# A new order for every operation of an attention + feed-forward kernel, and a last PSUM bank that is split

## The chip, the cores and the metric

The kernel runs on one core of a Trainium2 chip. The metric is the device time of one execution in microseconds (us): 369.22 us is the median of three runs of the kernel before (368.81, 369.22 and 369.6). One more execution was profiled; its own time was 369.51 us.

Names used below: TensorE (PE in the profile) multiplies matrices, its weight loads are PEld; VectorE is DVE, ScalarE is ACT, GpSimd is POOL, SyncE is SP. PSUM is the memory that TensorE writes, in banks of 2 KB per partition; SBUF is the large on-chip memory; HBM is off the core. A DMA moves data between HBM and SBUF and is issued from an engine's queue.

## The reference

```python
# attention, B=8 batches, H=12 heads, S=448 rows, D=64 columns per head
scores = (1/8) * q @ k.T
attn   = relu(scores)**2 / 448
y      = attn @ v                                   # [8, 12, 448, 64]
x      = y.transpose(0, 2, 1, 3).reshape(3584, 768)
# feed-forward, w_in [768, 2048], w_out [2048, 768]
h      = x @ w_in
g      = 0.5 * h * (1 + erf(h / sqrt(2)))           # exact gelu
out    = g @ w_out                                  # [3584, 768], float32
```

Inputs are float32 in HBM; matrices are cast to bf16 by the loads (or by a copy, for the first blocks), and sums are kept in float32 in PSUM.

## The kernel before, in words

**The work.** For each batch there are four kinds of TensorE work.

- *Transposes* (`T`): q and k come with their rows on the partitions and are wanted with D on the partitions. For batches 0 and 1 TensorE does this (`add_tk`, `add_tq`) into a bank `tp`, which ACT or DVE copies to SBUF. For batches 2 to 7 it is done by DMA transposes that are issued from SP's queue (`add_T_dma`); each waits for its load and for all scores of the batch two before, whose buffer it fills. Per batch there are three groups of four heads, and per group three transposes: k, the even and the odd part of q (called k, e and o below: T3.0k is batch 3, group 0, k).
- *Attention* (`A`): a score step (`add_steps`, 21 per batch) is four matmuls of 64x64 tiles into a two-bank tile `ps`; ACT or DVE applies the scaled relu, and DVE squares it into `a_sq`. Seven steps feed one value product (`add_av`, 28 matmuls of 64x64 tiles into `pav`, three per batch), which two copies put into `xT`.
- *W_in* (`F`): `add_f1` makes one block of 128 hidden columns for one batch, six matmuls of 128x128 tiles by 448 columns into `psh`, and ACT applies gelu. There are 16 blocks for each of batches 0 to 4. The last three batches use a form with seven products in place of eight (`add_blocks`, tiles `pb`, sums on DVE at L1028 into `part`). W_in is loaded in five pieces of 2, 2, 4, 4 and 4 blocks (win0 to win4), each by three DMAs; block 8 is the first of win3.
- *W_out* (also `F`): two tiles of 128 rows are done plainly (`add_plain`); the rest are 13 groups of 256 rows (`add_group`), again with seven products, p1 to p7, of eight matmuls by 384 columns each into three banks a, b, c of one pool. Products that follow each other in one bank accumulate, and between them DVE (or ACT) passes a partial sum out: in bank b p6, p7, p4 lead to v2, v3 and c21; in bank c p5 leads to c22 and p3 to c12. c21 and c22 are the left and right half of the second 128 rows, c11 and c12 those of the first. `store_rows` writes a tile of 128 rows to HBM in one or two DMAs.

**PSUM.** `w_pp` has three tiles of two banks (tag "w"; `ps` and `pav`), `f_pp` two tiles of one bank (tag "f"; everything else).

**The order.** Every operation, load and transpose is recorded as an `Op` with its dependencies. A string, `ORDER` (L83), then lists all of them: each word is an engine (P TensorE, A ACT, D DVE, G GpSimd's queue, S SyncE's queue) and the number of the op. `place` (L351) walks the string and issues each op on that engine, so the string settles the order on every engine and queue, and for copies and relus also which of ACT and DVE does them. A word Z issues a zero product (`add_fill`), which only keeps TensorE running. Before the order begins TensorE runs `SPIN` zero matmuls of 512 columns.

**Loads and gates.** All loads but the first two tiles are issued from GpSimd's queue. From batch 3 on a load reuses the buffer of the batch before; a *gate* (`add_gate`), a small GpSimd copy that reads the result of a group's transposes, stands ahead of the loads that overwrite what these transposes read. The start of the load order is

```text
k0.1 q0.1a v0.0 k0.2 [ident] q0.2a v0.1 v0.2 q0.b win0 win1 k1.0 q1.0 v1.0 win2
k1.1 q1.1 v1.1 win3 k1.2 q1.2 v1.2 win4 k2.0 q2.0 v2.0 k2.1 ...
```

Here k0.1 is k of batch 0, heads of group 1; q0.1a is the first half of the columns of q; q0.b the second half for all groups; [ident] is no load but the making of the identity matrix for TensorE's transposes, also on GpSimd. Later the gates of a batch alternate with loads: gate3.0 k4.0 q4.0 gate3.1 k4.1 q4.1 gate3.2 and so on.

Of the kernel before, what the change touches and what calls it, by code (L numbers as in the profile page):

```python
# [8 lines left out]
F32 = mybir.dt.float32  # L9
# [18 lines left out]
ND = DM // 2  # L28
# [51 lines left out]
SPIN = 9  # L80
# [3 lines left out]
G0 G1 G2 G3 G1429 G4 G5 A10 P11 D13 A16 G6 P17 D12 P14 D18 G7 P42 P39 P19 A15 G8 P21 D43 P33 D44  # L84
P36 A40 A22 D20 P54 P25 A37 P23 G9 D34 P51 D26 P48 A55 Z1024 D35 A24 D56 P69 Z672 D41 G117 A49
P57 D38 A52 P63 D70 P45 A58 D53 P66 D50 A64 P27 G118 A46 P31 D59 P60 D28 A67 D32 A47 P78 D65 P29
A61 P81 G119 D68 D30 A79 D62 G120 P93 P108 D71 A82 P84 A94 P75 D109 P72 G121 D83 A85 P90 D80
P129 G122 D73 A76 P105 A74 P102 G123 D95 D130 A91 G124 P131 D86 A106 P141 D77 D132 A103 D92 P111
P96 P165 D104 P143 A112 D107 D113 A97 P156 P87 D98 G125 A166 P99 D110 G126 A157 D88 P114 A142
G127 A89 D100 A101 P174 P168 G128 A144 P133 D115 P135 A116 P171 D175 P159 A169 D134 P251 D136  # L90
A160 D170 P145 D158 A172 A252 D167 P162 D176 P186 P192 A146 P243 D161 G147 D173 A187 G148 P253
A163 D193 G149 A244 D164 P195 G150 P180 P198 A254 P137 P139 G151 A181 D196 P183 P177 D138 A199
D140 A184 P189 P219 P245 D178 A190 D185 P247 D194 A220 G152 D179 A246 G153 P213 D188 P222 P204
D221 A248 G154 P263 D197 G155 A214 D200 P265 D191 A205 A264 D182 P261 A223 A266 D224 P216 P207
P201 S231 D206 A262 A208 P210 S229 P259 D209 A217 D215 P255 S232 D211 A260 P249 D212 D218 A256
D202 P225 A203 S228 A250 P257 A226 S230 P267 D227 A258 S234 P348 A268 P350 S233 G237 G238 A349
P352 G239 S235 A351 P354 S236 A353 P288 P294 P282 A355 P358 D289 P356 D283 A359 P360 D295 A357
D290 D296 P306 G240 A361 P279 G241 P276 P362 D307 P364 D280 A363 P366 D277 A365 P368 A367 P370
A369 P300 P285 P291 A371 P372 A292 D286 P374 D284 A373 P318 D301 P303 P312 A375 D308 P376 G242
G269 A304 D319 P378 G270 D278 A377 G271 P380 D313 G272 A379 D293 G273 D314 G274 P382 D390 A381  # L100
D305 D302 G275 D391 P330 P309 D287 D281 S398 P297 A331 D392 D320 S399 P315 P384 A298 D393 S401
A310 D396 A383 D417 P387 D394 A385 D419 A299 D311 A316 D395 P324 D317 P321 D418 A325 D397 P333
A388 P327 P421 D420 D322 S400 A328 P423 D323 A334 D326 S386 D422 P339 S402 P336 P342 D424 P425
D329 G407 G408 S403 A343 D335 P427 G409 A426 D337 S389 P429 A340 S404 D428 D344 P431 S405 D338
D341 P440 D332 P437 P345 D430 A438 D441 G410 P443 G411 P446 D432 P433 S406 A346 G412 D347 A444
P509 A447 D434 P511 D439 S435 D448 A510 S436 D442 P449 P452 P455 S541 D562 A512 P513 D445 A453
P515 D454 A450 A514 S542 P517 D456 G413 G414 D451 G415 P464 D457 S543 P461 P458 G416 A465 D462
A518 P467 P470 A516 P519 A459 P521 D471 A520 D472 P523 D466 A468 D460 A522 D560 P479 P476 P473
D469 A524 P525 D463 A477 P527 D480 A474 S544 D478 A526 P529 D475 A528 D481 P488 P485 P482 A489
D486 S545 A530 P494 P491 G550 P531 G551 D487 D483 G552 S546 P533 D495 A532 A484 P535 S547 D496  # L110
D561 A492 D490 A534 P503 P500 P497 D493 A536 P537 P564 D498 A538 D504 P539 A501 S548 D499 G553
A565 D505 G554 P600 D502 P603 G555 P506 S549 A601 D604 A540 P606 P609 P566 D563 A507 D602 P568
D607 D567 P570 D610 A569 A508 P572 G556 D571 G557 P624 P612 G558 P618 S704 P574 D580 G559 D608
A613 D573 P576 S705 A619 D581 D582 P627 D575 S706 P615 P584 D614 D577 A616 D611 P586 D605 A628
D617 A625 D620 P636 P630 A585 P621 D629 A631 D637 P633 P588 D587 A622 D626 D623 A634 S578 P639
P642 D583 P648 S707 P590 D638 G713 A640 D635 G714 A589 S579 D632 P592 G715 D641 A643 S708 D591
A649 P651 P657 D644 P645 S709 D593 A652 P666 D658 S710 P654 P594 D653 A646 D659 A655 D650 P596
A647 D667 D595 P660 P766 P663 D597 P672 A661 S711 D767 G716 P674 G717 A664 D662 A673 G718 D656
S712 P676 D668 A675 D665 S598 P772 P769 P669 S599 A770 D773 P763 A677 P775 P678 S867 D670 A764
D771 P680 D723 A776 D768 A679 S868 P790 A671 D765 P778 G719 P781 G720 A681 D777 P682 G721 S869  # L120
D791 P684 G722 D725 A683 P686 D779 A782 A685 D783 P688 D780 D774 P787 P793 D724 P784 A788 D794
A687 P799 P796 A689 P690 D795 D789 A797 P692 D798 A691 S870 P694 A693 A785 P696 A695 A786 P698
A800 S871 G876 A697 P802 G877 P811 D801 P805 A699 P700 G878 S872 A803 D812 P702 D792 A806 S873
D804 P814 D807 P817 P808 A815 D818 A701 P823 P820 A703 D816 P727 D809 A821 D726 P729 A810 D819
S874 A728 G879 D822 G880 D813 P826 A824 P829 G881 P906 S875 D730 P731 A830 D827 P733 A907 D828
D831 D825 P912 P921 P832 D745 A913 A732 P909 D922 P924 P735 D734 A833 A925 G882 P737 G883 A910
D743 G884 A834 D914 P936 P918 G885 P933 D736 P739 D738 S741 D744 A934 S978 P747 D908 A937 D740
S742 A919 D938 P749 S979 D935 A748 D926 P942 P930 S980 P915 D750 P751 A931 D943 P753 D920 A916
A752 D746 P755 D923 D911 D944 P948 P945 D917 P927 D888 S981 A949 D754 P939 D950 P757 A928 D886
D756 A946 P759 S982 D887 A940 D758 A929 P835 D932 S983 D947 D941 P957 P954 P951 S984 A836 A955  # L130
D958 P960 S985 P963 D760 P837 D959 A961 D952 S761 P839 D956 A953 S986 A838 D964 P966 P972 P969
D962 A840 P841 S762 D889 A973 D965 P843 A842 D967 P847 A970 A844 D971 P845 D968 D974 P990 P987
D1067 P975 A991 D988 A846 P993 P996 A848 D992 P849 A976 D1068 D1070 P851 A997 D989 A850 P853
A994 A977 D995 A852 P1005 P1002 P999 A854 P855 A1003 D1006 P859 D1004 A1000 D998 A856 P857 D1007
D1001 P1011 P1014 P1008 D1059 A858 A1012 D1015 P1017 P1026 P861 A1009 D1063 A860 P863 D1060
A1018 D1010 A1027 P1020 D1061 P1029 A862 P1023 P865 D1016 A864 D1019 A1021 D1028 P890 D1022 A866
P892 D1062 A1024 D1013 A891 D1025 P894 A1030 D1069 D893 D1031 P1035 P1038 P1032 A895 D1064 A1036
D1066 P1041 A1039 D1037 P1044 P896 D1033 A1042 D1034 A1045 P898 D1040 D1043 D897 P1047 D1046
P1050 P1053 D899 P900 D1139 A1048 D1049 P902 A1051 D1140 A1054 D1052 P1071 D1055 P1056 D901 S904
A1072 D903 S905 D1141 P1088 P1073 D1057 P1090 A1089 D1058 P1143 D1074 P1075 D1091 P1092 A1144  # L140
D1065 P1077 D1142 P1094 A1076 D1179 P1079 A1093 D1180 P1096 D1078 P1145 D1095 D1080 P1082 D1097
A1081 D1181 P1099 A1098 D1146 P1085 P1102 D1083 P1105 D1100 A1084 P1122 D1086 A1101 P1107 D1103
A1087 P1124 D1182 A1106 A1123 P1147 A1104 D1108 P1109 D1125 P1126 A1148 P1111 P1128 A1110 P1113
A1127 P1130 D1112 P1149 D1129 D1114 P1116 D1131 A1115 P1133 A1132 D1150 P1119 P1136 D1117 P1151
D1134 A1118 D1120 A1135 P1153 D1137 A1121 D1291 A1138 D1292 D1152 P1155 D1159 D1154 S1157 P1163
D1160 D1156 S1158 P1165 D1161 D1164 P1167 D1162 D1166 D1293 P1169 D1294 A1168 P1171 D1170 P1173
D1253 D1172 P1175 D1251 D1174 S1177 P1183 D1252 P1200 D1176 S1178 P1185 D1254 P1202 A1184 A1201
P1255 D1186 P1187 D1203 P1204 A1256 P1189 P1206 A1188 P1191 A1205 P1208 D1190 P1257 D1207 D1192
P1194 D1209 A1193 P1211 A1210 D1258 P1197 P1214 D1195 P1217 D1212 A1196 P1234 D1198 A1213 P1219
D1215 A1199 P1236 A1218 A1235 P1259 A1216 D1220 P1221 D1237 P1238 A1260 P1223 P1240 A1222 P1225  # L150
A1239 P1242 D1224 P1261 D1241 D1226 P1228 D1243 A1227 P1245 A1244 D1262 P1231 P1248 D1229 P1263
D1246 A1230 D1232 A1247 P1265 D1249 A1233 A1250 D1264 P1267 D1271 D1266 S1269 P1275 D1272 D1268
S1270 P1277 D1273 D1276 P1279 D1274 D1278 P1281 D1280 P1283 D1282 P1285 D1365 D1284 P1287 D1363
D1286 S1289 P1295 D1364 P1312 D1288 S1290 P1297 D1366 P1314 A1296 A1313 P1367 D1298 P1299 D1315
P1316 A1368 P1301 P1318 A1300 P1303 A1317 P1320 D1302 P1369 D1319 D1304 P1306 D1321 A1305 P1323
A1322 D1370 P1309 P1326 D1307 P1329 D1324 A1308 P1346 D1310 A1325 P1331 D1327 A1311 P1348 A1330
# [1378 lines left out]
```

## Time and profile before

| | |
|---|---|
| median of 3 runs | 369.22 us (368.81 to 369.6) |
| the profiled execution's own time | 369.51 us |
| its span in the trace | 367.7 us |
| mean granted TensorE clock | 0.993 |
| PE busy | 357.6 us, 97% of the span |
| PEld, DVE, ACT, POOL busy | 219.9, 285.4, 199.6, 64.4 us |
| last TensorE product ends | 362.6 us |
| last DMA lands | 366.5 us |

How to read it: all times inside the trace count from the span's start. The execution's time is 1.81 us above its span; 1.18 us of the span lie behind the last landing. A product whose results go on to DVE or ACT is free for them some 0.4 us after the end that the trace gives for its last matmul. Three stages follow one another in the span: the first 31 us, in which loads, transposes and the first batch's attention start up; up to about 249 us, in which attention of one batch and feed-forward work of earlier ones alternate on TensorE; and the rest, in which only feed-forward work is left.

### The profile page before, as it was taken

The numbers are of one execution on the slowest core, as the hardware profiler recorded it, in microseconds if no ns is written. First come the engines' busy times: TensorE is split into PE (matmuls) and PEld (weight loads), VectorE is DVE, ScalarE is ACT, GpSimd is POOL, SyncE is SP. The second block draws the span as 40 slices with busy tenths as digits, with TensorE's granted clock in tenths as the row PEclk, the third lists the DMA queues.
The fourth block names the chain that finished last, engine by engine and source line by source line (L and its number), as shares of the span: only waits on it lengthen the run. The fifth ranks groups of instructions, "written<-read, shape, count | busy, mean of one in ns | idle before, by whom it ended". The sixth has DMA issues, their size and how long they took to land.

```text
span 367.7 us, 8379 instructions
## 1 busy us (share of the span) xinstructions
PE 357.6 (97%) x3525; PEld 219.9 (60%) x3525; DVE 285.4 (78%) x473; ACT 199.6 (54%) x319; POOL 64.4 (18%) x103
## 2 busy tenths in 40 slices
PE   7899999999999999999999999999999999999995
PEld 3676644455554455545455544558875897688663
DVE  4898863699888889989598997998788558665862
ACT  5898954436467546775777568863540353045200
POOL 8566404140113240230402000000000000000000
PEclk9899999999999999999999999999999999999998
DMA  9999999999999999999998990002002301210323
GB/s 175 192 181 202 203 199 157 195 203 197 165 214 244 153 186 210 224 184 146 150 130 147 193 180 11 0 2 87 3 0 87 86 2 51 87 37 0 87 86 86
DMA packets 89540, 47.25 MB, mean 128 GB/s; under 512 B 55328, under 2 KB 86048, under 8 KB 89504
## 3 DMA queue, kind: packets, MB, share of 16 engines
q0 software_dynamic: 32912, 22.47, 43.6%
q1 hardware_dynamic: 55952, 23.76, 35.2%
q8 instruction: 27, 0.44, 0.5%
q10 hardware_dynamic: 640, 0.51, 0.4%
q14 instruction: 9, 0.07, 0.1%
HBM read 45.61 MB, written 11.01 MB: 154 GB/s over the span
## 4 chain that ended last, share of the span: by engine, by line
PE 92%; ACT 2%; DVE 2%; DMA 2%; POOL 1%; issue 1%; DVEq 0%; POOLq 0%; ACTq 0%
PE pso L1164 32%; PE psh L847 26%; PE pb L991 13%; PE ps L734 10%; PE pav L795 8%; PE pso L1259 3%; ACT a_sq L746 2%; DMA nq<-in_q_dram 2%; DVE part L1028 1%; PE tp L605 0%; POOL nk L546 0%; PE tp L633 0%; DVE xs L958 0%; DVE a_sq L748 0%; DVE osb L1198 0%
## 5 line engine op out<-in xcount | busy, mean ns | idle before, releaser
L746 ACT ACTIVATE a_sq<-ps 128x896 bf16<-128x896 f32 (+1 forms) x119 | 104.5, 918 | 36.6 <-PE ps L734 36.4
L755 DVE TENSOR_TENSOR a_sq<-a_sq 128x896 bf16<-128x896 bf16 (+1 forms) x169 | 96.9, 616 | 9.0 <-ACT a_sq L746 8.3
L847 PE MATMUL psh<-xT,win_sb 128*128 128x448 bf16 (+1 forms) x516 | 96.2, 340 | 0.1
L847 PEld LDWEIGHTS <-win_sb 128*128 128x128 bf16 x516 | 48.1, 98 | 45.3 <-issue 9.2
L748 DVE TENSOR_SCALAR a_sq<-ps 128x896 bf16<-128x896 f32 (+1 forms) x50 | 53.4, 1077 | 17.3 <-PE ps L734 17.2
L857 ACT ACTIVATE h_sb<-psh 128x448 bf16<-128x448 f32 x80 | 43.2, 548 | 29.1 <-PE psh L847 28.9
L1164 PEld LDWEIGHTS <-s_sb 128*128 128x128 bf16 x424 | 40.7, 98 | 26.7 <-issue 2.1
L1028 DVE TENSOR_TENSOR part<-pb,part 128x448 f32<-128x448 f32 x60 | 34.6, 619 | 21.5 <-PE pb L991 21.5
L734 PE MATMUL ps<-qT,kT 64*64 64x448 bf16 (+1 forms) x756 | 49.0, 342 | 1.5 <-ACT a_sq L746 1.2
L1164 PEld LDWEIGHTS <-h_sb 128*128 128x128 bf16 x312 | 29.6, 98 | 21.9 <-issue 3.8
L1164 PE MATMUL pso<-wout_sb,s_sb 128*128 128x384 bf16 (+2 forms) x216 | 38.1, 320 | 0.1
L1164 PE MATMUL pso<-wout_sb,h_sb 128*128 128x384 bf16 x208 | 38.1, 327 | 0.0
L1164 PE MATMUL pso<-t_sb,s_sb 128*128 128x384 bf16 x208 | 38.1, 326 | 0.0
L795 PE MATMUL pav<-a_sq,v_sb 64*64 64x448 bf16 (+1 forms) x756 | 36.5, 329 | 0.4 <-issue 0.3
L734 PEld LDWEIGHTS <-kT 64*64 64x64 bf16 x756 | 19.4, 108 | 22.8 <-issue 16.8
L1037 ACT ACTIVATE h_sb<-part 128x448 bf16<-128x448 f32 x36 | 20.1, 578 | 20.2 <-DVE part L1028 19.9
L1198 DVE TENSOR_TENSOR osb<-pso,p_sb 128x384 f32<-128x384 f32 x39 | 21.6, 555 | 10.0 <-PE pso L1164 7.4
L991 PEld LDWEIGHTS <-win_sb 128*128 128x128 bf16 x288 | 27.6, 98 | 2.3 <-issue 0.4
L795 PEld LDWEIGHTS <-v_sb 64*64 64x64 bf16 x756 | 21.2, 107 | 11.6 <-issue 1.4
L701 POOL COPY gate<-qT 128x16 bf16<-128x16 bf16 x15 | 5.3, 350 | 109.8 <-DMA qT<-nq 108.8
L991 PEld LDWEIGHTS <-ws 128*128 128x128 bf16 x216 | 20.7, 98 | 0.0
L1145 DVE TENSOR_TENSOR s_sb<-h_sb 128x1024 bf16<-128x1024 bf16 x26 | 17.8, 683 | 2.3 <-PE pso L1164 2.3
(61 smaller groups left out, 292.6 us busy)
## 6 DMA issues: line engine op xcount, KB each, us to landing
nk<-in_k_dram POOLq DMA_DIRECT2D x23, 224.0 KB, 7.9
nq<-in_q_dram POOLq DMA_DIRECT2D x21, 224.0 KB, 8.9
v_sb<-in_v_dram POOLq DMA_DIRECT2D x5, 672.0 KB, 11.2
out_dram<-osb SPq DMA_DIRECT2D x8, 336.0 KB, 3.7
v_sb<-in_v_dram POOLq DMA_DIRECT2D x9, 224.0 KB, 8.0
out_dram<-osb SPq DMA_DIRECT2D x7, 288.0 KB, 4.3
out_dram<-osb SPq DMA_DIRECT2D x8, 240.0 KB, 3.1
win_sb<-in_moe_w_in_dram POOLq DMA_DIRECT2D x8, 192.0 KB, 8.9
```

What stands on the lines that cost most here:

```text
L734: nc.tensor.matmul(ps[64 * j : 64 * j + 64, e, x * w : x * w + w], kT[r, g, i * 128 + 64 * j : i * 128 + 64 * j + 64], moving, start=True, ...
L746: A.activation(ar, ps, AF.Relu, scale=c_att)
L748: V.tensor_scalar(ar, ps, c_att, 0.0, op0=mybir.AluOpType.mult, op1=mybir.AluOpType.max,)
L755: V.tensor_mul(box["a2"][:, :, :used], ar, ar)
L795: nc.tensor.matmul(pav[0][o2 : o2 + 64, e, :w], vt[b][r, 2 * g + e, bass.ts(i, D)], box["a2"][r, y, o : o + w], start=(i == 0), stop=(i == ...
L847: nc.tensor.matmul(ph[:, x * n : x * n + n], win_sb[:, kd, bass.ts(m + x, 128)], xT[b][:, kd, c], start=(kd == 0), stop=(kd == KD - 1),)
L857: A.activation(h_ring()[:, m : m + nm, o + c.start : o + c.stop], box[0][:, :S].rearrange("p (x n) -> p x n", x=nm), AF.Gelu,)
L991: nc.tensor.matmul(bank[name][:, y, z * HS : z * HS + HS], w[:, k, bass.ts(mm, 128)], right()[:, k], start=first and k == 0 and z == 0, st ...
L1028: V.tensor_add(get(to), ps(name), get(other))
L1037: A.activation(h_ring()[:, m : m + 2, o + half[c].start : o + half[c].stop], src().rearrange("p (x n) -> p x n", x=2), AF.Gelu,)
L1164: nc.tensor.matmul(box[bank][:, n0:n1], left()[:, kf], right()[:, kf, n0:n1], start=bool(need) and kf == 0, stop=kf == K2 - 1, skip_group_ ...
L1198: V.tensor_add(out()[:, n0:n1], box[bank][:, n0:n1], other()[:, n0:n1])
```

## The change

`SPIN` goes from 9 to 10, and the whole string `ORDER` is replaced: 1430 words become 1432. The ops are the same but for the last group, described below, so nothing is computed otherwise; what differs is order and place.

- **TensorE.** The same products in another order. A change between attention (64x64 tiles) and feed-forward products (128x128 tiles) comes 46 times each way in the order before and 55 and 56 times in the new one. The zero products become 480 and 448 columns instead of 1024 and 672, and stand a few ops later. TensorE's transposes of batches 0 and 1 stand in longer runs in places.
- **ACT and DVE.** ACT has 298 ops instead of 317, DVE 490 instead of 470: five relus, eight passes of groups, four x copies, two plain copies and one copy of transposed k go from ACT to DVE, and one op is new.
- **Loads.** The order on GpSimd's queue becomes

```text
k0.2 q0.1a k0.1 q0.2a q0.b [ident] v0.0 v0.2 q1.0 v0.1 k1.0 k1.1 win1 q1.1 win0 win2
v1.1 v1.0 win3 k1.2 q1.2 win4 q2.2 k2.0 q2.0 q2.1 k2.1 v1.2 k2.2 v2.0 gate2.1
wout0 wout1 gate2.0 wout2 v2.2 k3.1 gate2.2 q3.1 q3.2 q3.0 v2.1 k3.0 v3 k3.2 ...
```

and from there on the gates of a batch come together, with the next batch's loads in a burst behind them.

- **SP's queue.** The transposes of a batch come in another order among themselves (batch 2: 0k 0e 0o 2k 2e 1e 1o 1k 2o; batch 3: 0e 0o, then the store of the first plain tile, then 0k 1k and the rest; batch 4: 0o 0k 0e 2o 1o 2k, two stores, 1k), and stores stand at other places among them.
- **The last group.** p5, c22, p3 and c12 come in two parts of 256 and 128 columns. The part of 128 has a bank of its own, "d", out of the pool with tag "w". The order of the end was p7, p5, p4, p3 (256), p3 (128), with c12's 128 columns and a small store of them last, on ACT's and SP's queues. It becomes p7, p5 (128), p5 (256), p3 (128), p3 (256), p4, with c21 (384 columns) and the store of the second 128 rows, full width, last, on SP's queue.

```diff
-SPIN = 9
+SPIN = 10
 ORDER = """
-G0 G1 G2 G3 G1429 G4 G5 A10 P11 D13 A16 G6 P17 D12 P14 D18 G7 P42 P39 P19 A15 G8 P21 D43 P33 D44
-P36 A40 A22 D20 P54 P25 A37 P23 G9 D34 P51 D26 P48 A55 Z1024 D35 A24 D56 P69 Z672 D41 G117 A49
+G3 G1 G0 G4 G7 G1431 G2 A10 P11 D13 A16 G6 P17 D12 P14 D18 G118 P42 P39 P21 D15 P23 G5 A43 P36
+D22 P33 G117 A40 P19 D24 P25 D44 G121 A34 D20 G9 Z480 P54 P48 D41 A37 P51 D26 Z448 D38 A55 P63
...
-P1391 D1386 D1390 P1393 D1392 P1395 D1394 P1397 D1405 D1396 P1399 D1403 D1398 S1401 P1407 D1404
-D1400 S1402 P1409 D1406 D1408 P1411 D1410 P1413 D1412 S1423 P1415 D1414 P1417 D1416 P1419 D1418
-S1424 P1420 D1421 S1425 D1422 S1426
+A1308 D1374 A1325 P1377 A1334 A1311 D1376 A1328 P1379 D1383 D1378 S1381 P1387 D1384 D1380 S1382
+P1389 D1385 D1388 P1391 D1386 D1390 P1393 D1392 P1395 D1394 P1397 D1396 P1399 D1403 D1398 S1401
+P1407 D1404 D1400 S1402 P1409 D1408 P1411 D1406 D1405 D1410 P1413 D1412 S1425 P1416 P1415 D1414
+D1418 P1422 D1417 P1421 D1424 S1428 P1419 D1423 S1427 D1420 S1426
 """
...
-                if need:
+                if need and bank == "d":
+                    box[bank] = w_pp.tile([128, 2, NB], F32, tag="w", name="psd")[:, 0]
+                elif need:
                     box[bank] = f_pp.tile([128, NB], F32, tag="f", name="pso")
...
-        p5 = product("c", lambda: box["s", 1], lambda: tsum(1), [s1, s2], need=("f",), frees=("s1",))
-        c22 = passed("c", part(1, right), part(1, right), [v3, p5])
+        ends = [("c", 0, ND)] if g < NG - 1 else [("c", 0, LAST), ("d", LAST, ND)]
+        p5 = [
+            product(
+                x, lambda: box["s", 1], lambda: tsum(1), [s1, s2],
+                need=("f",) if x == "c" else ("w",), n0=n0, n1=n1,
+            )
+            for x, n0, n1 in ends
+        ]
+        p5[-1].frees = ("s1",)
+        c22 = [
+            passed(x, part(1, right), part(1, right), [v3, o], n0=n0, n1=n1)
+            for o, (x, n0, n1) in zip(p5, ends)
+        ]
...
-        ends = [(0, ND)] if g < NG - 1 else [(0, LAST), (LAST, ND)]
         p3 = [
-            product("c", lambda: box["s", 4], lambda: quad[1, 1], [c22, s4], n0=n0, n1=n1)
-            for n0, n1 in ends
+            product(x, lambda: box["s", 4], lambda: quad[1, 1], [o, s4], n0=n0, n1=n1)
+            for o, (x, n0, n1) in zip(c22, ends)
         ]
...
-        c12[-1].frees = ("f",)
+        c12[0].frees = ("f",)
+        if g == NG - 1:
+            c12[1].frees = ("w",)
```

More of the change, by code (lines that the diff above doesn't have):

```diff
@@ L89 @@
[L89 to L100, printed above, removed]
@@ L161 @@
[L161 to L162 removed]
+G3 G1 G0 G4 G7 G1431 G2 A10 P11 D13 A16 G6 P17 D12 P14 D18 G118 P42 P39 P21 D15 P23 G5 A43 P36
+D22 P33 G117 A40 P19 D24 P25 D44 G121 A34 D20 G9 Z480 P54 P48 D41 A37 P51 D26 Z448 D38 A55 P63
+P27 P29 A49 D52 P57 D28 P81 A64 D35 P69 P31 D53 G122 A58 P45 D30 D65 A82 P75 G8 D50 P131 D32 A70
+P66 D59 A76 P93 D56 D46 A67 P60 D77 D47 A94 P84 P108 D71 P129 A61 G120 D68 A62 P78 D95 A109 P72
@@ new lines @@
+P1041 A858 P1017 P861 D1028 A1009 D1068 A1018 D1010 P890 D1031 A862 D1059 P1053 A1042 P1020
+P1050 D891 P865 D1013 A1021 D1019 P894 D1022 A1054 D1025 A1051 P1035 D1016 P1038 A866 P1032
+D1060 A1039 D1043 P1044 P892 D1062 A1033 D1034 A1045 P1071 D1070 P1088 D893 P896 D1036 A1089
+A895 D1049 P1073 A1072 D1179 P1090 D1069 P1079 D1040 P1092 D1055 P1096 D1074 D1052 P1077 P898
+D1061 D1141 P1075 D897 P900 D1091 D899 D1180 P902 D1078 D1064 P1082 D1046 P1094 A1093 D1080
+P1085 A1076 D1037 P1056 D1083 D1139 D1095 P1099 D903 A1057 P1143 D901 S904 A1058 D1100 S905
@@ L1231, in add_group @@
         c12 = [
-            passed("c", part(0, right), part(0, right), [o], n0=n0, n1=n1)
-            for o, (n0, n1) in zip(p3, ends)
-        ]
-        c12[-1].frees = ("f",)
+            passed(x, part(0, right), part(0, right), [o], n0=n0, n1=n1)
+            for o, (x, n0, n1) in zip(p3, ends)
+        ]
+        c12[0].frees = ("f",)
+        if g == NG - 1:
+            c12[1].frees = ("w",)
         if g < NG - 1:
-            sch.add((("SP", 0.6, 2.8),), store(1, full, [nc.sync] * 2), [c22, c21], frees=("osb",))
+            sch.add((("SP", 0.6, 2.8),), store(1, full, [nc.sync] * 2), c22 + [c21], frees=("osb",))
             sch.add((("SP", 0.6, 2.8),), store(0, full, [nc.sync] * 2), [c11] + c12, frees=("osb",))
@@ L1240, in add_group @@
             sch.add((("SP", 0.6, 2.8),), store(0, left, [nc.sync] * 2), [c11])
-            sch.add((("SP", 0.6, 2.8),), store(1, full, [nc.sync] * 2), [c22, c21])
-            for o, (n0, n1) in zip(c12, ends):
+            sch.add((("SP", 0.6, 2.8),), store(1, full, [nc.sync] * 2), c22 + [c21])
+            for o, (_, n0, n1) in zip(c12, ends):
                 c = slice(ND + n0, ND + n1)
@@ L1246, in add_group @@
             readers.setdefault(bb, []).extend(mine)
-        return [(1.3, o) for o in (p1, p6, p2, p7, p5, p4)] + [(1.3 / len(p3), o) for o in p3]
+        split = 1.3 / len(ends)
+        return (
+            [(1.3, o) for o in (p1, p6, p2, p7)] + [(split, o) for o in p5] + [(1.3, p4)]
+            + [(split, o) for o in p3]
+        )
     plain = []
```

127 lines of the change are left out of this document (65 added, 62 removed).

## Prediction

> **What bounds the kernel now.** I read the page's first two parts, then the chain of waits, then windows of the start, and the timeline and DMA issues of the places that the change touches.
>
> The page:
>
> ```profile
> span 367.7 us, 8379 instructions
> PE 357.6 (97%) x3525; PEld 219.9 (60%) x3525; DVE 285.4 (78%) x473; ACT 199.6 (54%) x319; POOL 64.4 (18%) x103
> PE   7899999999999999999999999999999999999995
> PEclk9899999999999999999999999999999999999998
> DMA  9999999999999999999998990002002301210323
> PE 92%; ACT 2%; DVE 2%; DMA 2%; POOL 1%; issue 1%; DVEq 0%; POOLq 0%; ACTq 0%
> ```
>
> TensorE is the bound: busy 97% and 92% of the chain. Only the first slices and the last have idle time or a low clock. Between them a new order can win only what TensorE still waits for, or lose by making its products longer or late.
>
> The chain in order of time (start, us, what) gives prices of runs and two waits, the ACT and DVE pieces:
>
> ```profile
> 106.72 0.69 PE ps L734 x12
> 107.41 3.51 PE psh L847 x18
> 163.18 2.38 PE psh L847 x12
> 166.25 4.64 PE psh L847 x24
> 241.09 1.74 ACT a_sq L746 x2
> 271.11 2.30 DVE part L1028 x4
> ```
>
> Windows of the start (window, length, busy of PE, PEld, DVE, ACT, POOL with counts, granted clock, DMA share, GB/s) and the PE wait that stands in the first of them:
>
> ```profile
> PE tp L633 <- DMA nq<-in_q_dram: 1.6, 2, 1.4
> 8.87:10.26 1.39, 0.00 (x0) 0.00 (x0) 0.56 (x1) 1.16 (x2) 1.18 (x3) 1.00 1.38 194
> 10.75:14.15 3.40, 3.40 (x55) 2.54 (x50) 3.24 (x6) 2.63 (x3) 1.83 (x3) 0.50 1.61 189
> ```
>
> TensorE stands idle until the fifth load has landed, at 10.22; the clock then reads 0.50 for 3.4 us.
>
> Timeline and DMA issues of win3, and the tail (the first two lines end in us to landing after issue):
>
> ```profile
> 25.52 0.63 POOL L486 DMA_DIRECT2D win_sb<-in_moe_w_in_dram  x1 [1.66 <-DMA win_sb<-in_moe_w_in_dram]
> win_sb<-in_moe_w_in_dram POOLq DMA_DIRECT2D x1, 192.0 KB, 9.3
> 363.21 0.62 DVE L1198 TENSOR_TENSOR osb<-pso,osb 128x256 f32<-128x256 f32 x2 [0.76 <-PE pso L1164]
> out_dram<-osb SPq DMA_DIRECT2D x1, 336.0 KB, 2.9
> out_dram<-osb SPq DMA_DIRECT2D x1, 48.0 KB, 2.5
> ```
>
> **The change part by part.** The sum is made on the profiled execution: 369.51 us, its span 367.70 and 1.81 outside it. It lies 0.29 above the median, so 0.29 comes off at the end.
>
> *The start.* The first DMA for q's group 2 goes from fifth to fourth of the queue: it landed at 10.22, behind loads that landed at 8.26 and 9.53, about 1.2 us apart. I put it at about 9.0, which closes most of the idle 1.39 us. The identity moves behind five load issues instead of four, some 0.4 us, and the tenth warm-up product covers 0.4 us. q0.b goes from ninth to fifth (15.85 to about 12.4), win1 is near 21, and win0 moves behind it to about 24, so the first feed-forward block, at 22.93 before, starts later. Zero products lose 768 columns, 0.3 us at full clock. What all this is worth is decided where the two orders have done the same work: at the product of block 8, which needs win3. It ran at 35.37. The third DMA of win3 was issued at 25.52 and took 9.3, so it landed at 34.84, and the same set of loads stands ahead of win3 in both orders. ACT and DVE have equal work up to batch 0's last x copy (ACT 21.1 us in both; DVE 20.5 and 20.7). So the new product starts between 34.9 (the landing) and 35.37 (nothing gained); I take 35.1, −0.27. Work before it differs by one score step more: 0.19 less is left after it.
>
> *Switches.* Behind block 8 the new TensorE order has 51 alternations of attention and feed-forward, the old one 43. A run of two blocks takes 2.38, of three 3.51, of four 4.64: 1.13 a block and 0.11 once per run. A run of two score steps takes 0.50, of three 0.69: 0.19 a step and 0.12 once per run. So a pair of switches costs 0.11 + 0.12 = 0.23, and eight pairs 1.84. Nothing hides this, as TensorE has no idle time here. Bounds: zero, if the constant is the pipe's modelled end and not a cost; against that, products after 31 us stand end to end and their sum follows the clock time within 0.5 us over 200 us. Above, 8 x (1.45 − 1.32) for value products that stand alone adds up to 1.0. The rows measure the switch itself, so I take 1.84.
>
> The trace shows the constant wherever 64x64 and 128x128 products meet. [...]
>
> *Stalls that go.* Two waits of TensorE after 31 us are tied to the old order: 0.36 at 242.9 (a score step waits for ACT's relus, the chain's "241.09 1.74 ACT") and 0.24 at 274.9 (a product waits for a copy held behind DVE's block sums, "271.11 2.30 DVE"). In the new order the releasing ops stand early enough. −0.35 and −0.23, together −0.58. Next late there would be ACT's gelus, with over 0.5 us to spare.
>
> *Moved ACT and DVE ops.* 20 more on DVE. DVE is 78% busy and ACT 54%. By the rows' durations (relu 0.92 on ACT, 1.08 on DVE; square 0.62) I followed each TensorE op's release in the new order: beyond 35 us none comes after TensorE is ready for it, apart from the last group. Cost 0, covered by TensorE's own products; if that cover fails at a place, a wait like the two above, 0.2 to 0.4, comes back, up to 0.8 in all.
>
> *SP and GpSimd queues.* Transposes, stores, loads and gates change places; every one issues and reads the same bytes. Gates in runs hold loads of a batch until its last group is transposed, but q and k of a batch are asked for some 25 us later. The DMA transposes land 3.0 to 14.9 us after issue. By the old trace's landings (about 0.8 us apart once the loads have drained) and its score steps, batch 2's first comes at about 52.5 for a need at 54.5; T3.0k, behind a store of a plain tile, is issued near 92, lands near 96.5 and is needed at 99.6; T4.0 at 121 for 126. I take 0; upper bound 4.1 (rival 2).
>
> *The last group.* One product of 384 columns becomes 256 + 128: +8 matmuls, no more columns, 0. The p3 part of 256 columns must wait for c22's part, with only p3's 128 columns (0.43) between: an estimated +0.23. The tail: before, the last product's end was at 363.0 for DVE, its 128-column pass ended at 363.83, and the last landing was at 366.52, 3.52 behind the product. After, the pass has 384 columns: 0.20 to start and 0.56 to run, and the store of a whole row tile then took 3.32 from DVE's end to landing at 362.45 (issue 0.38 with two DMAs on one queue, 2.9 to land). 0.20 + 0.56 + 3.32 = 4.08, +0.56. Bounds: 0 (the small DMA took 2.5 too) to +1.0.
>
> *Sum.* TensorE's end: 363.0 − 0.27 − 0.19 + 1.84 − 0.58 + 0.23 = 364.0. Span: 364.0 + 4.08 + 1.18 (last landing to end, as before) = 369.3. With 1.81: 371.1; less 0.29: **370.8**, +1.6 on the median.
>
> **The rivals.**
>
> *1. The start wins more than the switches cost (faster).* The other terms, +1.84 − 0.58 − 0.19 + 0.23 + 0.56 = +1.86, less the forecast's −0.27, are paid back when block 8 starts at 33.5; faster by 0.2% needs 32.8, 2.6 us earlier. For it: the idle 1.39 and the half clock behind it (3.40 busy at 0.50, worth 1.7 at full clock) make 3.1 together, and both follow one late load. Against it: win3's landing and the queue ahead of it, and ACT and DVE, whose work alone reaches about 34.1. It decides if the loads up to win3 go 2 us faster in the new order. At 32.6 the time is 368.3. The same side is reached if the switch costs nothing: 370.8 − 1.84 = 369.0, no change.
>
> The trace has a half clock of 3.4 us behind a gap of only 1.39. [...]
>
> *2. Transposes come late (slower).* T3.0k issued at 92.2 can take 3.1 to 11.4 us (11.4: a transpose issued at 84.77 that landed at 96.14, in the trace of before): up to 4.1 late for the steps at 99.6. For it: the loads are now in bursts, and transposes land only once outstanding loads have drained. Against: 7.4 us are left for it, where the median transpose takes 6.0 to 6.6 in that stretch. It decides from 7.4 us on; 1 to 4.1 late gives 371.8 to 374.9.
>
> *3. W_in later (slower).* win1 and win0 are swapped and stand behind q1.0, k1.0 and k1.1; if feed-forward work that filled TensorE's first 35 us is missing and attention cannot fill it, block 8 starts at 36.6 or later: 372.3.
>
> *4. No change.* The start returns all (33.5), or half of the switches' 1.84 is hidden and half of these 1.6 is won (370.8 − 0.92 − 0.8): about 369.2.
>
> **How the numbers follow.** About 0.2% (0.74 us) is what a measurement can tell from no change. Main forecast 0.44 (its own range 369.9 to 371.9: switches at 0.85 to 2.8, small stalls up to 0.4); rival 3 0.12 and rival 2 0.08, both slower; rival 1 0.20; rival 4 0.16. Slower 0.64, same 0.16, faster 0.20. Range: rival 1's 368.3 just inside at the low end, at the top rival 3 with some of rival 2: 368.2 to 373.0.
>
> **What would show it.** Block 8's first product near 35.1 and no idle stretch before 10.3; the same lengths per run but 51 pairs behind it; no wait of TensorE on a transpose; ACT and DVE no longer in the chain at 241 and 271; last product's end near 364, a full-row store last, landing some 4.1 behind it. I would be wrong by the start if block 8 comes at 33.5 or before, by the switches if the run lengths change, and by the queues if TensorE waits for qT or kT.

## The result, and the profile after

The changed kernel takes 370.82 us (median of 7 runs, 370.5 to 371.14), the kernel before 369.58 us in the same set (median of 7, 368.45 to 370.15). The ratio is 1.0038, with a 95% interval of 1.0023 to 1.0053: slower by 0.9 to 2.0 us. Medians and ranges are of all runs, while ratios and intervals leave out the executions more than 1.5% above the fastest of their kernel. The profiled execution of the changed kernel took 370.67 us, its span is 368.9.

The page of the changed kernel, its first two parts and the shares of the chain of waits:

```profile
span 368.9 us, 8397 instructions
PE 359.5 (97%) x3532; PEld 218.2 (59%) x3532; DVE 295.6 (80%) x493; ACT 187.9 (51%) x300; POOL 62.6 (17%) x103
PE   8799999999999999999999999999999999999994
PEclk9999999999999999999999999999999999999999
PE 94%; DVE 3%; DMA 1%; ACT 1%; issue 0%
```

TensorE is the bound as before, with 1.9 us more busy time; ACT has 11.7 us less and DVE 10.2 more, and neither shows in the total. No slice has a lower clock now.

Windows of the start (columns as in the prediction) show that the idle stretch and the half clock are gone:

```profile
8.87:10.26 1.39, 0.87 (x35) 0.82 (x30) 1.29 (x3) 1.39 (x2) 1.39 (x3) 1.00 1.73 188
10.75:14.15 3.40, 2.81 (x77) 1.81 (x72) 3.39 (x7) 3.40 (x5) 1.27 (x2) 1.00 1.33 201
```

Block 8's first product began at 34.68 us, 0.69 ahead of the 35.37 in the profile of before. From there to the end of the kernel's last DVE pass (364.56; 363.83 before) it is 329.88 us against 328.46, 1.42 more, and from there to the end of the span 4.3 against 3.9, 0.4 more. Together 1.1 us, which is the growth of the span before rounding.

The chain in order of time (start, us, what), three lines of the stage between 100 and 130 us and then the end; behind it two lines of the timeline there, and the last store among the DMA issues (KB, us to landing):

```profile
105.79 0.69 PE ps L734 x12
106.48 1.24 PE psh L847 x6
107.72 0.50 PE ps L734 x8
...
361.16 0.44 DVE osb L1200
361.59 0.04 issue
361.63 2.35 PE pso L1166 x16
```

```profile
364.00 0.56 DVE L1200 TENSOR_TENSOR osb<-pso,p_sb 128x384 f32<-128x384 f32 x1 [0.87 <-PE pso L1166]
364.59 0.31 SPq L1125 DMA_DIRECT2D out_dram<-osb  x1
```

```profile
out_dram<-osb SPq DMA_DIRECT2D x1, 336.0 KB, 2.8
```

A run of one block takes 1.24 here, as 1.13 + 0.11; there are more of such short runs. From 361.16 to 361.60 the chain runs through a DVE pass, c22's part of 256 columns; the product that starts at 361.63, p3's 256 columns, waits for it. The last pass has 384 columns and is followed by the full-row store.

### The profile page after: what moved, and what is told of

It reads as the page before. It is cut to its first block, busy times and chain, and to the rows that moved or that the text cites. A ratio compares the mean times of both kernels' runs of the same rounds, so it can differ in the third digit from the quotient of the medians.

```text
span 368.9 us, 8397 instructions
## 1 busy us (share of the span) xinstructions
PE 359.5 (97%) x3532; PEld 218.2 (59%) x3532; DVE 295.6 (80%) x493; ACT 187.9 (51%) x300; POOL 62.6 (17%) x103
## 4 chain that ended last, share of the span: by engine, by line
PE 94%; DVE 3%; DMA 1%; ACT 1%; issue 0%
PE pso L1166 32%; PE psh L847 26%; PE pb L991 13%; PE ps L734 10%; PE pav L795 9%; PE pso L1277 3%; DVE a_sq L755 1%; DMA q<-in_q_dram 1%; ACT a_sq L746 1%; PE tp L605 1%; DVE qT L511 0%; PE tp L633 0%; DVE a_sq L748 0%; DVE osb L1200 0%; ACT nq L513 0%
## 5 line engine op out<-in xcount | busy, mean ns | idle before, releaser
L746 ACT ACTIVATE a_sq<-ps 128x896 bf16<-128x896 f32 (+1 forms) x114 | 100.2, 921 | 29.9 <-PE ps L734 29.7
L847 PE MATMUL psh<-xT,win_sb 128*128 128x448 bf16 (+1 forms) x516 | 97.3, 340 | 0.0
L748 DVE TENSOR_SCALAR a_sq<-ps 128x896 bf16<-128x896 f32 (+1 forms) x55 | 58.9, 1078 | 24.7 <-PE ps L734 24.6
L1028 DVE TENSOR_TENSOR part<-pb,part 128x448 f32<-128x448 f32 x60 | 35.6, 619 | 7.4 <-PE pb L991 5.5
L1166 PE MATMUL pso<-wout_sb,s_sb 128*128 128x384 bf16 (+1 forms) x208 | 37.7, 324 | 0.1
L1166 PE MATMUL pso<-t_sb,s_sb 128*128 128x384 bf16 (+1 forms) x208 | 37.7, 324 | 0.0
L734 PEld LDWEIGHTS <-kT 64*64 64x64 bf16 x756 | 18.6, 105 | 24.7 <-issue 19.9
L1037 ACT ACTIVATE h_sb<-part 128x448 bf16<-128x448 f32 x36 | 18.6, 571 | 21.2 <-DVE part L1028 12.7
L701 POOL COPY gate<-qT 128x16 bf16<-128x16 bf16 x15 | 3.7, 247 | 111.5 <-DMA qT<-nq 111.5
L1200 DVE TENSOR_TENSOR osb<-pso,osb 128x384 f32<-128x384 f32 (+1 forms) x26 | 14.1, 544 | 7.8 <-PE pso L1166 7.5
```

The costliest lines, as they stand in the source:

```text
L734: nc.tensor.matmul(ps[64 * j : 64 * j + 64, e, x * w : x * w + w], kT[r, g, i * 128 + 64 * j : i * 128 + 64 * j + 64], moving, start=True, ...
L746: A.activation(ar, ps, AF.Relu, scale=c_att)
L748: V.tensor_scalar(ar, ps, c_att, 0.0, op0=mybir.AluOpType.mult, op1=mybir.AluOpType.max,)
L847: nc.tensor.matmul(ph[:, x * n : x * n + n], win_sb[:, kd, bass.ts(m + x, 128)], xT[b][:, kd, c], start=(kd == 0), stop=(kd == KD - 1),)
L1028: V.tensor_add(get(to), ps(name), get(other))
L1037: A.activation(h_ring()[:, m : m + 2, o + half[c].start : o + half[c].stop], src().rearrange("p (x n) -> p x n", x=2), AF.Gelu,)
```

## The experiments

Each kernel is compared with the kernel before on the same chip; the runs of before were pooled in four sets and gave medians of 369.63 (29 runs), 368.99 (17), 369.36 (23) and 368.95 (22); the last two sets come from one chip. In each set its runs lie 2.5 to 7.6 us apart, so differences from it are good to some 0.7 us at best.

### The last group undone

```diff
-P1407 D1404 D1400 S1402 P1409 D1408 P1411 D1406 D1405 D1410 P1413 D1412 S1425 P1416 P1415 D1414
-D1418 P1422 D1417 P1421 D1424 S1428 P1419 D1423 S1427 D1420 S1426
+P1407 D1404 D1400 S1402 P1409 D1408 P1411 D1406 D1405 D1410 P1413 D1412 S1423 P1415 D1414
+P1417 D1416 P1419 D1418 S1424 P1420 D1421 S1425 D1422 S1426
```

> The changed kernel with the last group and its order as before (p5 whole, p4, then p3 in 256 + 128 columns, the small store last). Theory: the last group costs 0.26 us for the product that waits for c22's part and 0.4 us for the later full-row store, so this kernel lies 0.65 below the changed one, that is 0.5 to 0.7 above before (369.6 gives about 370.2). Rival: the last group costs nothing that can be seen, and the kernel stays 1.2 above before.

Measured: 370.04 us (12 runs, 369.83 to 371.36), ratio to before 1.0016 (0.9997 to 1.0036); the changed kernel had 1.0038 in its own set. That is 0.78 us below the changed kernel by medians of two sets, which alone is no more than a hint. The traces are sharper: this one has no wait of a product on c22, and the changed kernel needs 0.24 us more from block 8 to the end of the last product and 0.44 more from there to the end of the span. The last group costs about what the forecast gave it (0.23 + 0.56), the tail a little less.

### New start, old rest; old start, new rest

The first kernel takes the words of the new order up to the value product P177 (about 37 us) and then every other word in the order of before; the second the other way round, with the seam at P189 (about 36 us). Both have the old last group. Extracts of the words at the seams:

```diff
 # new start, old rest
-SPIN = 9
+SPIN = 10
-G0 G1 G2 G3 G1429 G4 G5 A10 P11 D13 A16 G6 P17 D12 P14 D18 G7 P42 P39 P19 A15 G8 P21 D43 P33 D44
+G3 G1 G0 G4 G7 G1429 G2 A10 P11 D13 A16 G6 P17 D12 P14 D18 G118 P42 P39 P21 D15 P23 G5 A43 P36 D22
...
+P186 A254 P137 D164 G151 P139 D161 A190 G150 P177 G127 A187 G149 P183 D138 A199 D140 A184 P219 P245
```

```diff
 # old start, new rest
-D140 A184 P189 P219 P245 D178 A190 D185 P247 D194 A220 G152 D179 A246 G153 P213 D188 P222 P204
+G150 P180 P198 A254 P137 P139 G151 A181 D196 P183 P177 D138 A199 D140 A184 P189 D182 G154 A190 P213
```

> The new order of all engines and queues up to the 191st word (a value product of batch 1, at some 37 us), and behind it every op in the order of before, with the old last group. Theory: the start of the new order wins 0.7 us at block 8 and one score step (0.19), and nothing behind it takes this back: 0.9 below before, about 368.7. Rival: the start of the profiled executions differs by the clock at 10 to 14 us only, which is no property of the order, or the gain is lost behind the seam: 0 to 0.3 below before.

> The order of before up to the 196th word (a score step of batch 1, at some 36 us), and behind it the new order, with the old last group. Theory: eight more pairs of switches cost 1.84, two stalls that are gone return 0.58, so 1.2 to 1.5 above before, about 371.0; with the new start (0.9) and the new last group (0.65) the three parts add up to the change. Rival: the switches are not what costs; then this kernel lies at before or below it by up to 0.6, and the loss of the change is in its start and end.

Measured: new start and old rest 368.99 us (12 runs, 368.75 to 370.92), ratio 0.9987 (0.9967 to 1.0007); old start and new rest 369.96 (12 runs, 369.35 to 372.94), ratio 1.0021 (0.9996 to 1.0047).

Two things follow. First, the kernel of the last section and this one with the new start differ in the rest alone, were run on one chip, and most of their runs lie within 0.6 us: 370.04 − 368.99 = 1.05 us is the price of the new rest. The forecast had 1.84 − 0.58 = 1.26. Second, the start does not behave as an amount that is added. Block 8 began at these times:

| profiled kernel | start | block 8, us | its time, us |
|---|---|---|---|
| before, first profile | old | 35.37 | 369.51 |
| old start, new rest | old | 34.25 | 370.74 |
| changed kernel | new | 34.68 | 370.67 |
| new order, old last group | new | 35.11 | 370.38 |
| new start, old rest | new | 34.88 | 368.95 |

The old start without half clock is faster than the new one. Its gain was not kept: the execution with 34.25 is one of the slower ones of its kernel, with 330.16 us from block 8 to the end of the last product where the same rest behind the new start has 329.04. (For the median of this kernel the expectation was a miss by 1 us, as it counted from a start at 35.37.) Of these 1.12 us, 0.19 is the score step that the new start has already done by block 8. The rest is one wait of TensorE, the first line here; the second line is a wait of DVE:

```profile
PE ps L731 <- DMA qT<-nq: 0.9, 1, 0.9
```

```profile
DVE osb L1195 <- DMA out_dram<-osb: 0.9, 1, 0.9
```

The first is a score step of batch 4 at 126.7 us, 0.93 us late, that waits for T4.0e, which landed at 126.53; in the new order with the new start the same transpose landed 1.45 us ahead of its step, in the changed kernel 2.3. The second, at 98.4 us, is for the store of the first plain tile; no product of TensorE came late by it.

### Sixteen more pairs of switches

In the kernel before, neighbouring TensorE words were exchanged at 16 places between 60 and 140 us, for instance

```diff
-F1.3 | Q2.0.4
+Q2.0.4 | F1.3
-F2.4 | Q3.1.1
+Q3.1.1 | F2.4
...
```

(F1.3 is block 3 of batch 1, Q2.0.4 score step 4 of batch 2, group 0.)

> The kernel before with 16 neighbouring pairs of TensorE ops exchanged between 60 and 140 us, each where a run of feed-forward products meets a run of attention, so that 16 more pairs of switches arise and nothing else changes. Theory, by the run lengths of before: 16 x 0.23 = 3.7 us longer, about 373.3. [...] If the constant per run is only how ends are modelled: 0.

Measured: 372.51 us (6 runs, 371.91 to 373.86), ratio 1.0093 (1.0066 to 1.0120). The traces give the price without the start: from block 8's first product to the end of the last product the kernel before has 327.80 us, this one 331.49, which is 3.69 us for 16 pairs, 0.231 per pair. By medians it is 2.88 (2.4 to 4.4 by the interval), less sharp, as the starts differ too. Followed op by op, the difference grows by about 0.23 at each of the 16 places and nowhere else. The chain of this run in order of time shows the short runs that arose:

```profile
107.48 0.50 PE ps L731 x8
107.98 1.24 PE psh L844 x6
109.22 0.32 PE ps L731 x4
109.54 1.24 PE psh L844 x6
```

The price by run lengths holds (3.7 expected, 3.69 measured).

### The first 19 loads exchanged

The new order (with the old last group) with the loads of before up to win3, and the kernel before with the new loads up to win3; nothing else changes. The two orders, in words:

```diff
 # GpSimd's words in the kernel before: k0.1 q0.1a v0.0 k0.2 ident q0.2a v0.1 ...
+# k0.2 q0.1a k0.1 q0.2a q0.b ident v0.0 v0.2 q1.0 v0.1 k1.0 k1.1 win1 q1.1 win0 win2 v1.1 v1.0 win3
```

> The new order with the old last group, and the first 19 loads and the identity (up to win3) in the order of before. Theory: the load order is what makes the start of before late and uneven; with q0.2a and q0.b late again TensorE stands idle near 9 to 10 us and the times spread over 2 us or more, median 0.3 to 1.0 above the kernel with the new loads (370.04), about 370.6. Rival: the order of TensorE, ACT and DVE makes the start even, and the loads do nothing: 370.0 with a spread under 1 us.

> The kernel before with only its first 19 loads and the identity in the new order. Theory: q0.2a lands at 8.7 instead of 10.2 us, the idle stretch at 8.9 to 10.3 goes, win0 comes about a microsecond late for block 0, and the times stand close together: median 368.6 to 369.0, spread under 1 us. Rival: the median and the spread of before (369.6, over 2 us) stay.

Measured: 376.09 us (5 runs, 375.86 to 377.35) and 371.11 us (6 runs, 370.91 to 371.86), ratios 1.0196 (1.0173 to 1.0219) and 1.0059 (1.0040 to 1.0078). Neither expectation held. TensorE's waits of the first show over 4 us for q, behind which the clock reads 0.50 for 3.41 us (block 8 begins at 40.88); those of the second, the identity and W_in, are only 1.0 us together (block 8 at 37.73):

```profile
PE tp L630 <- DMA nq<-in_q_dram: 4.7, 2, 4.2
```

```profile
PE tp L630 <- POOL ident L1316: 0.7, 1, 0.7
PE psh L844 <- DMA win_sb<-in_moe_w_in_dram: 0.3, 1, 0.3
```

The second kernel's late start has more to it. In its trace the granted clock first reads 1.00 from a record at 13.6 us, where the others at full clock have that record at 3.8 to 6.2, and until then a row of 16 score products takes 0.96 us instead of 0.58:

```profile
12.42 0.96 PE L731 MATMUL ps<-qT,kT 64*64 64x224 bf16 x16
19.30 0.58 PE L731 MATMUL ps<-qT,kT 64*64 64x224 bf16 x16 [0.38 <-ACT a_sq L743]
```

TensorE was busy for 7.2 us between 5.0 and 13.6, at the lower rate. The profiled execution is also the slowest of the six (371.86, the others 370.91 to 371.34), and whether the others had the same slow clock is not on record. So load order and engine order belong together in the start: the old loads under the new order cost about 6 us (376.09 against 370.04 on another chip), nearly all of it by block 8 (40.88 against 35.11). The new loads under the old order cost 2 (371.11 against 368.99), but how much of that is waits and how much the clock stays open.

### The idle stretch filled, and the kernel before once more

```diff
-P36 A40 A22 D20 P54 P25 A37 P23 G9 D34 P51 D26 P48 A55 Z1024 D35 A24 D56 P69 Z672 D41 G117 A49
+P36 A40 A22 D20 P54 Z3072 P25 A37 P23 G9 D34 P51 D26 P48 A55 Z1024 D35 A24 D56 P69 Z672 D41 G117 A49
```

> The kernel before with zero products of 3072 columns (1.3 us) in the idle stretch ahead of the transposes of q's group 2, nothing else. Theory 1: the stretch of half clock (3.4 us at 0.50, which the profile of before shows and those of the two other kernels with the old start do not) is what makes before uneven and costs 1.1 to 1.3 us at block 8; filled, the clock stays at 1.00 and the median falls to 368.2 to 368.7. Theory 2: only few executions have the half clock (granted clock 0.993 and less in 1 of 29), and the spread has another cause: 369.6 as before, spread over 2 us.

> The kernel before unchanged, for a second profile. If the half clock belongs to its start, block 8 begins near 35.4 again and the window 10.75 to 14.15 reads 0.50; if not, block 8 begins near 34.1 to 34.3, as in the two other kernels with its start, and the execution is 1.1 to 1.3 us shorter than 369.5 unless something later is late.

Measured: with the stretch filled 369.65 us (12 runs, 368.32 to 371.96), ratio 1.0017 (0.9994 to 1.0040); its window 8.87 to 10.26 has TensorE busy for all of 1.39 and the clock at 1.00. Theory 1 fell: the half clock is not what makes the kernel before uneven. In that profile block 8 began at 34.45.

The second profile of before, at 369.30 us, is the one that explains most. Its windows of the start:

```profile
8.87:10.26 1.39, 0.54 (x16) 0.29 (x18) 0.90 (x1) 1.39 (x2) 1.32 (x3) 1.00 1.42 198
10.75:14.15 3.40, 2.53 (x52) 1.42 (x52) 3.40 (x7) 3.27 (x5) 1.70 (x3) 1.00 1.62 189
```

TensorE is busy in part of the first stretch, there is no half clock, and block 8 began at 33.92, 1.45 us ahead of the first profile. Yet the last product ended at 362.94 instead of 363.17: 1.2 of the 1.45 us were given back. The offset between TensorE's start times and the sum of its work (how far its products have slipped) grows at 98.3 us (0.36), 101.9 (0.31) and 153.5 (0.51), where the first profile has no wait. DVE's waits and the timeline name the cause of the first two:

```profile
DVE osb L1198 <- DMA out_dram<-osb: 2.4, 2, 1.6
```

```profile
97.68 0.56 DVE L1198 TENSOR_TENSOR osb<-pso,p_sb 128x384 f32<-128x384 f32 x1 [1.62 <-DMA out_dram<-osb]
```

DVE waits 1.62 us for a free output buffer: the store of the first plain tile, whose data was ready at 86.59, stands in SP's queue behind T3.0o and T3.1k. T3.1k's issue alone took 6.09 us (84.56 to 90.65), the store was issued at 93.21 and landed at 97.56. In the first profile it landed at 97.85, hardly elsewhere: in these two profiles the DMAs set this time, and a faster start only comes to it earlier. The third step comes 2.6 us behind a wait of DVE of 0.74 for a group's store, at 150.9; that the one follows from the other is not shown. The kernel with the stretch filled met the first store harder: it landed at 99.12, DVE waited 2.7 us and TensorE stood 1.4 us at 99.85, more than the 0.92 us by which its block 8 was ahead of the first profile. In the changed kernel the store stands ahead of T3.0k, was issued at 90.82 and landed at 95.30; its trace has no wait on a store at all.

### What the late store is worth

In SP's order of the kernel before the store was put ahead of T3.0o and T3.1k, which also change places; then, in a second kernel, the score step that waits at 242.9 us was put behind the next product too.

```diff
-T3.0k T3.0e T3.1k T3.0o store(plain 0) T3.1e
+T3.0k T3.0e store(plain 0) T3.0o T3.1k T3.1e
 # the second kernel, TensorE
-Q7.2.2 Q7.2.3 | p(b) p(c) | Q7.2.4
+Q7.2.2 | p(b) | Q7.2.3 | p(c) | Q7.2.4
```

> The kernel before with one thing moved: on SP's queue the store of the first plain tile stands ahead of T3.0o and T3.1k instead of behind them. Theory: where the start goes well (block 8 near 34.0), DVE waits up to 2.7 us near 96 us for this store, and TensorE for DVE, which gives the start's gain back; the store then lands 2 to 6 us earlier, this wait goes, and the median falls by 0.5 to 1.0 to 368.2 to 368.7, with fewer executions above 369.5. Rival: the store is one of several things that the DMAs pace, the next (transposes of batch 3, the store near 150 us) takes its place, and median and spread stay as before.

> The same, and the score step that waits at 242.9 us for ACT's relus moves behind the next product. By the prices of this study a wait of 0.36 to 0.41 goes and one pair of switches (0.23) comes: 0.15 to 0.2 below the kernel with the store ahead alone, about 368.2. Rival: the step is late again in its new place, or the next one is: no difference.

Measured: 369.48 us (12 runs, 368.52 to 375.42), ratio 1.0013 (0.9982 to 1.0044), and 369.26 us (12 runs, 368.21 to 528.21) with a ratio of 0.9988 (0.9962 to 1.0014). In the first kernel's profile (368.74) the store landed at 95.10, the wait near 97 is gone and DVE waits for a store once, 0.7 us near 150; TensorE slips 0.50 us at 152.9. The median did not move: the rival holds, or the spread has another source. The second kernel's gain of 0.2 by medians cannot be told from none. Its 528.21 us is the profiled execution: the clock was granted at 0.65 from 5.2 us to the end (mean 0.656 over the span), and the other eleven runs end at 371.16. So no profile shows this kernel at its usual clock, and what caused that execution is open.

Two further kernels put the pieces together: the new start with the rest of before and two waits removed (also a DVE sum moved behind the pass c22 that it held up at 274 us), and the kernel before with the stretch filled, the store ahead and the same two waits removed. The edit to DVE's order:

```diff
 # words of TensorE and DVE alone
-D1137 D1291 D1292 D1152 P1155 D1159 D1154
+D1137 D1291 D1152 P1155 D1159 D1154 D1292
```

> The kernel with the new start, the rest of before and the last group of before, and two waits taken away: the score step that waits at 242.9 us stands behind the next product, and a DVE sum of block inputs (xs, the second of its batch) stands behind the pass of a group instead of ahead of the pass before. Theory: 0.18 for the first (0.41 less a pair of switches, 0.23) and 0.24 for the second, so 0.4 below the new start with the rest of before (368.99 then), about 368.6, and faster than both kernels by 0.8 and 2.2. Rival: each wait turns up again a few products later: 369.0.

> The kernel before with the idle stretch filled by zero products, the store of the first plain tile ahead of T3.0o and T3.1k, and the same two waits taken away. Theory: if the idle stretch with its half clock and the late store are what makes the kernel before uneven, nearly all executions lie at the fast end less 0.4: median 367.8 to 368.3. Rival: the spread has a further cause that these profiles do not hold: the fast end falls by 0.4 to about 367.8 and the median stays near 369.

Measured: 368.88 us (12 runs, 368.24 to 372.34), ratio 1.0002 (0.9973 to 1.0030), and 370.44 us (12 runs, 368.08 to 376.96), ratio 1.0022 (0.9996 to 1.0049). In both profiles the two waits are gone. The fast end of the first fell by 0.5 from that of the new start alone (368.75, on another chip), as the two waits promised, but its median cannot be told from that of before. Its profile, an execution of 371.47 us, shows the store again, now with the new start (block 8 at 35.20); the waits of DVE and of TensorE:

```profile
DVE osb L1195 <- DMA out_dram<-osb: 3.0, 1, 3.0
```

```profile
PE pso L1161 <- DVE osb L1195: 1.6, 1, 1.6
```

TensorE stood 1.6 us at 101.4. So the old rest is exposed to this store with either start. The order on SP's queue helps: with the store ahead it landed at 95.1 to 95.9 in four profiles, and with the old order at 97.0 to 100.7 in seven. It is no full guard, as the kernel with the old start and the new rest has the changed kernel's order there, and its store landed at 98.24. The second kernel, with the store ahead and the stretch filled, is as uneven as the others: nine of its runs end at 371.69 (median 369.36), three took 375.52 to 376.96. What else makes the kernel before uneven stays open; apart from the kernel with the old loads and the execution of 528.21, no profile holds an execution of 372 us or more. None of the kernels is shown to be faster than before.

## Why the prediction was right, and where it was not

*The time.* Forecast 370.8, measured 370.82; the interval of the measured move, 0.9 to 2.0 around +1.24, holds the forecast +1.6. The closeness to the last digit is luck, since the median of before is 0.36 higher over seven runs than over the three that the sum was set against, and the terms have errors that cancel. The path was right: TensorE sets the time, switches cost more than the removed stalls return, and the last group adds to it.

*Switches: right.* Term 1.84 for eight pairs. The profile with 16 added pairs gave 0.231 per pair against 0.23 taken from the chain, and the orders do differ by eight pairs behind block 8 (51 against 43). The 0.85 at the low end of the forecast's own range is a term that no run shows; by the measured price eight pairs cost 1.85. From block 8 to the end of the last product the changed kernel needs 1.48 us more in the traces, where the terms 1.84 − 0.19 − 0.58 + 0.23 give 1.30.

*Stalls that go: right for the two that the profile showed.* The changed kernel's TensorE has no step in its offset at 242 or 275 us. But the step was incomplete: in a quick execution the kernel before has three more (0.36, 0.31, 0.51), two because of a store that the first profile does not show as a wait, the third probably so. The new rest costs 1.05 us on one chip where the two terms gave 1.26.

*The last group: right.* Forecast +0.23 and +0.56, and 0.78 less without it. In the trace the wait on c22 is 0.24, and from the last product's DVE pass to the landing it is 3.2 us where 3.32 was taken. The base of this sum was misread: the trace of before ends the last product at 363.17, not at 362.6 or 363.0, and DVE's last pass in the changed kernel starts 0.04 us after the trace's end of its product (363.97), where 0.4 and another 0.20 were taken. Over the trace of before, DVE and ACT ops that waited for a product started a median 0.04 us after its end (91 and 108 waits). With that base the last product came 0.80 us later, where the sum had 1.0, and the stretch from it to the end of the span grew by 0.34, where the sum had 0.56.

*The start: the step that failed.* The term was −0.27 at block 8 (and −0.19 for one step done earlier), measured from 35.37. Three of its facts held: q's group 2 landed at 8.68 (9.0 expected), the idle stretch and the half clock went, win1 and win0 came at 20.74 and 23.41. win3 landed at 33.94, 0.9 before the floor that I had taken from the profile, and block 8 began at 34.68. It was no floor: in the second profile of before, with the old loads, win3 landed at 33.55. (q0.b, by the way, was the eighth load of before, not the ninth.) But 35.37 was the odd value: four further profiles with the old start have 33.92, 34.06, 34.09 and 34.25, so the new start is 0.4 to 1.3 us later (34.68 to 35.20 in four profiles). A mean granted clock as low as that profile's 0.993 stands in only 5 of the 91 pooled runs of before. So the term took one execution's half clock for a property of the order. Whether the new start is worth anything to the median is not shown (0.64 us below before, 0.9967 to 1.0007). If it is, the traces suggest why: the old start's lead is lost behind it, at stores and transposes whose landings the DMAs set. But putting the store ahead did not lower the median, so this is argued and not shown.

*Rival 1 (start wins more than 2.6 us):* did not come; what was named against it, ACT's and DVE's work up to 34.1, nearly stands: in no profile here does block 8 begin before 33.92. *Rival 2 (transposes late):* not in the changed kernel, where T3.0k was issued at 91.73 and landed at 96.01 (92.2 and 96.5 expected); with the old start in front one did come late, 0.93 us at T4.0e. That transposes land only once outstanding loads have drained is too strong: of those issued with loads still out, 36 of 39 in the trace of before and all 20 in the changed kernel's landed behind the last of these loads, but T3.0k of before landed at 91.38, ahead of a load that was issued before it and landed at 93.29. The plain tile's store ahead of T3.0k was counted as a risk; that it also lands earlier there, 95.30 against 97.6 to 97.9 in the two profiles of before, was overlooked, as the moved queue words were costed at zero. *Rival 3 (W_in later):* no.

*Moved ACT and DVE ops:* zero was right; the only wait of TensorE for them past 35 us is the one on c22.

## What to carry to other kernels

Price a reorder of TensorE by how often it changes tile shape: 0.23 us for each return trip here, confirmed by adding such trips and nothing else. One profile is one execution: before a start-up term is taken from it, look whether a second execution has the same stalls, above all where the runs are 1 to 2 us apart. Of a lead of 1.45 us at block 8, 1.2 was gone by the last product here, 0.67 of it at one late store; look for what stands behind a slow issue on the same queue.

## What the runs showed of the hardware

- Ahead of the last product the clock fell to 0.50 in two profiles, for 3.41 us each time: after an idle stretch of 1.39 us in the first profile of before, and after one of 4.19 us in the kernel with the old loads. In the profile with 16 more switches the stretch of 1.39 us had TensorE busy for 0.22 of it, and in the second profile of before for 0.54, and the clock stayed at 1.00 in both. In the 3.41 us just before the fall, as long as the fall itself, TensorE was busy for 1.73 us in the one (first line below) and 0.11 in the other (second line). Two falls do not give a threshold.

```profile
7.31:10.72 3.41, 1.73 (x58) 1.17 (x54) 2.11 (x5) 2.72 (x4) 3.20 (x6) 1.00 1.33 187
18.11:21.52 3.41, 0.11 (x4) 0.11 (x6) 2.28 (x6) 0.29 (x1) 3.15 (x5) 1.00 1.33 202
```

- In one execution of more than 200 on record the granted clock stood at 0.65 from 5.2 us to the end (mean 0.656 over the span), and it took 528.21 us.
- The issue of a single DMA transpose held SP's queue for 6.09 us, where the two ahead of it took 1.2, and a store behind it, ready since 86.59, left at 93.21. In the first profile of before the same issue took 5.90, with the stretch filled 6.24.
- Exchanging two orders of the same first 19 loads cost 2.1 us (371.11 against 368.99) and 6.1 (376.09 against 370.04) where the engines' order stayed, though the bytes are the same and all go through one queue.
